# Linear attention, soft mixture of experts, ELU network: expert weights loaded by halves during the attention

## Chip, cores and metric

The kernel runs on one core of a Trainium2 chip. The metric is device time in microseconds, the median of several executions. The profile and the trace are those of one execution.

## The reference, cut to what matters

Three stages follow one another. The change touches the loads of `w1` and `w2`, which the second stage reads.

```python
# 1. linear attention: B, H, S, D = 4, 8, 768, 48
for t in range(S):
    cur = einsum('bhd,bhe->bhde', u * k[t], v[t])
    y[t] = einsum('bhd,bhde->bhe', r[t], state + cur)
    state = w * state + einsum('bhd,bhe->bhde', k[t], v[t])
# 2. soft MoE: x is 3072 x 384, 8 experts with 4 slots each, F = 1024
logits = x @ phi
d = softmax(logits, over tokens);  c = softmax(logits, over slots)
slot_input = d.T @ x
for e in range(8):
    slot_out[e] = relu(slot_input[e] @ w1[e]) @ w2[e]   # w1: 384x1024, w2: 1024x384
x = c @ slot_out
# 3. feed forward: 384 -> 2048 -> 384, w_in and w_out given as 64-bit floats
out = elu(x @ w_in) @ w_out
```

## The kernel before

The attention is computed in chunks of 128 rows, 24 of them (six for each of the four batches). One Python loop, `for s in range(-2, NCH)`, writes out the instructions of each step by hand, and every engine runs its own part of that list in order. In step s the kernel finishes chunk s, computes the scores of chunk s + 1 and prepares the keys of chunk s + 2. A step begins on TensorE with `update(s + 1)`, 16 small products at line 569 that read the values `vd` of chunk s + 1. They can therefore be used to see where a step begins. VectorE scales the keys, turns and masks the scores, adds the rows together and shifts bits in the conversion of `w_in` and `w_out` from 64-bit to 32-bit floats. The conversion (`wide_load`, `wide`) takes one piece of 384 columns in each of steps 0 to 19, through a scratch buffer `scr` of four pieces. The mixture's logits and slot sums for groups of four chunks are interleaved as `extras`.

All loads of this loop leave from SyncE's queue (SP), in the order in which the step lists them: `load_k(s + 4)`, after the keys of chunk s + 2 are scaled, as there are two key buffers; `load_v(s + 3)`; `wide_load(s + 2)`, one transfer of 384 KB or two smaller ones; `load_r`, 384 KB in every second step; and, at the end of some steps, weights of an expert. Keys and values are 192 KB in rows of 192 bytes, `r` is in rows of 384 bytes. The values of chunk s + 3 are thus asked for in step s and first read at the beginning of step s + 2.

There are sixteen expert matrices `we0` to `we15`: eight `w1`, each 128 x 3 x 1024 on the chip, and eight `w2`, each 128 x 8 x 384; 1.5 MB (12 KB per partition) apiece. The pool `we_p` has ten buffers, one of which is `scr`. The nine others take `we0` to `we8` during the attention. A whole matrix is issued at the end of steps 0, 3, 5, 7, 10, 12, 14, 17 and 19. The buffer is treated as 3072 columns, and a half of it is 1536. A half of a `w1` matrix does not end at the end of one of its three blocks of 1024 columns, so `load_half` (line 369 and line 374) needs two transfers for it: four for a matrix, of 512, 256, 256 and 512 KB, in rows of 4, 2, 2 and 4 KB. A half of a `w2` matrix is one transfer of 768 KB in rows of 1.5 KB. The rule for the step is:

```python
            if s >= 0 and s * (NWE - 1) // (NP + 1) >= nwe and nwe < NWE - 1:
                load_we(nwe, we_p)
                nwe += 1
```

with NWE = 10 and NP = 20. `we9` and the halves of `we10` follow in steps 21 and 22, the others after the attention, when buffers come free. After the attention `up` multiplies the slot inputs with four `w1` at a time (line 1048) and `down` with four `w2` (line 1070); both find a block through `we_at`.

Of the kernel before, what the change touches and what calls it, by code (L numbers as in the profile page):

```python
# [236 lines left out]
def kernel(  # L237
# [14 lines left out]
    nc = tc.nc  # L252
    B, H, S, D = r.shape
    E, DM, FE = w1.shape
# [7 lines left out]
    KD = DM // 128  # L262
    KF = FE // 128
# [15 lines left out]
    NWE = 10  # L279
    we_p = main.enter_context(tc.tile_pool(name="we_p", bufs=NWE, side="right"))  # L280
# [16 lines left out]
    for a in range(2):  # L297
# [5 lines left out]
        out=mask, in_=mask, compare_op=ALU.is_gt, fill=0.0, base=0, pattern=[[1, 128]], channel_multiplier=-1  # L303
# [45 lines left out]
    we = {}  # L349

    HW = KD * FE // 2

    def load_we(i, pool, part=None):
        if part in (None, 0):
            t = pool.tile([128, 2 * HW], F32, tag="we", name=f"we{i}")
            we[i] = [t[:, :HW], t[:, HW:]]
        for h in range(2) if part is None else [part]:
            load_half(i, h)

    def load_half(i, h):  # L360
        n = FE if i < E else DM
        src = (w1[i] if i < E else w2[i - E]).rearrange("(k p) f -> p k f", p=128)
        at = 0
        while at < HW:
            k, c = divmod(HW * h + at, n)
            m = min(HW - at, n - c)
            if c == 0 and m == n:
                m = (HW - at) // n
                nc.sync.dma_start(
                    out=we[i][h][:, at:at + n * m].rearrange("p (k f) -> p k f", k=m), in_=src[:, k:k + m]  # L370
                )
                at += n * m
            else:
                nc.sync.dma_start(out=we[i][h][:, at:at + m], in_=src[:, k, c:c + m])
                at += m

    def we_at(i, at, n):
        h, o = divmod(at, HW)
        return we[i][h][:, o:o + n]


# [16 lines left out]
    with ExitStack() as actx:  # L398
# [123 lines left out]
        def load_v(n):  # L522
            b, c = divmod(n, NC)
            vd[n] = at2.tile([128, H, D], F32, tag="vd", name="vd", bufs=4)
            nc.sync.dma_start(out=vd[n], in_=v[b, :, C * c:C * c + C, :].rearrange("h p d -> p h d"))

        def scale(n):
            nc.vector.tensor_tensor(out=km[:, :, 0:D], in0=rk.pop(n), in1=wk, op=ALU.mult)
# [37 lines left out]
        def update(n):  # L566
            for p in range(HP):
                for a in range(2):
                    nc.tensor.matmul(
                        out=pu[64 * a:64 * a + D, p, :], lhsT=km[:, 2 * p + a, 0:D], rhs=vd[n][:, 2 * p + a, :],  # L570
                        start=True, stop=True,
                    )
# [29 lines left out]
        def state(n):  # L602
            c = n % NC
            if c == NC - 1:
                return
            if c == 0:
                nc.vector.tensor_copy(out=t1, in_=pu)
            else:
                nc.vector.tensor_tensor(out=t1, in0=qc, in1=pu, op=ALU.add)
            nc.gpsimd.tensor_tensor(out=qc, in0=t1, in1=w128.unsqueeze(2).to_broadcast([128, HP, D]), op=ALU.mult)  # L610
# [73 lines left out]
        def logits(j, g0=0, g1=G):  # L684
            if g0 == 0:
                lg[j] = pm_p.tile([128, 128], F32, tag="pm", name="ps_l")
            for kk in range(KD):
                for g in range(g0, g1):
                    nc.tensor.matmul(
                        out=lg[j][32 * g:32 * g + 32, :], lhsT=phi_sb[:, kk, :], rhs=xT[G * j + g][:, kk, :],  # L690
                        start=(kk == 0), stop=(kk == KD - 1),
                    )
# [70 lines left out]
        def part(j):  # L763
            fs = [[logits], [slots_a], [], [slots_b], [slots_c], [slots_d], [slots_e], [slots_f], [], [], [], []]
            fs = [[(f, j) for f in l] for l in fs]

            def stage(l):
                for f, i in l:
                    f(i)

            return [lambda l=l: stage(l) for l in fs]
# [43 lines left out]
        NP = -(-NW // PW)  # L815
# [30 lines left out]
        def wide(j, f):  # L846
            if 0 <= j < NP:
                raw, a = piece(j)
                if f is not wide_d:
                    f(raw, a)  # L850
                    return
                merged = []
                for o, at, i, c, p, m in spans(j):
                    if merged and merged[-1][0] == o:
                        merged[-1][3] += m
                    else:
                        merged.append([o, at, p, m])
                for o, at, p, m in merged:
                    wide_d(raw[:, at:at + m, :], a[:, at:at + m], (wov if o else wiv)[:, p:p + m])
# [18 lines left out]
        load_r(1)  # L878
        load_k(1)
        load_v(1)  # L880
        nwe = 0
        extras = [lambda: None] * 7 + [flags_a, lambda: None, lambda: None, flags_b, lambda: None, flags_c, flags_d]

        def extra():
            if extras:
                extras.pop(0)()
# [3 lines left out]
        for s in range(-2, NCH):  # L890
            now, nxt, ahead = s >= 0, 0 <= s + 1 < NCH, s + 2 < NCH
            last = s == NCH - 1
            if nxt:
                update(s + 1)
            wide(s, wide_a)
            if last:
                extra()
                extra()
                extra()
                logits(GS - 1, 0, G - 1)  # L900
            else:
                extra()
            if s > 0 and s % G == 0:
                extras += part(s // G - 1)
            if nxt:
                state(s + 1)
            if ahead and s > -2:
                scale(s + 2)
            if 2 <= s + 4 < NCH:
                load_k(s + 4)  # L910
            if 2 <= s + 3 < NCH:
                load_v(s + 3)
            if s < 1:
                wide_load(s + 2)
            if now:
                for p in range(HP):
                    rows_a(s, p)
                rows_b(s)
                wide(s - 1, wide_d)
                if s >= 1 and s + 2 < NP:  # L920
                    wide_load(s + 2)
            if nxt:
                for p in range(HP):
                    scores(s + 1, p)
                causal(s + 1, 0)
                bonus_a(s + 1)
                bonus_c(s + 1)
            if not last:
                extra()
            turn_r(s + 3, k0 if s == -2 else rp)  # L930
            if s == -2:
                tables_b()
            if nxt:
                causal(s + 1, 1)
            if s % 2 == 0 and s // 2 + 3 < NCH // 2:
                load_r(s // 2 + 3)
            if now:
                x_T(s)
            if last:
                logits(GS - 1, G - 1, G)  # L940
            if nxt:
                bonus_b(s + 1)
            if ahead:
                ps = turn_k(s + 2)
            if nxt:
                bonus_d(s + 1)
            for f in (wide_b1, wide_b2, wide_b3):
                wide(s, f)
            if ahead:
                cross(s + 2, ps)  # L950
            wide(s, wide_c)
            if nxt:
                state_b(s + 1)
            spread(s + 4)
            if s == NCH - 2:
                warm(3)
            extra()
            if nxt:
                for p in range(HP):
                    before(s + 1, p)  # L960
            if s >= 0 and s * (NWE - 1) // (NP + 1) >= nwe and nwe < NWE - 1:
                load_we(nwe, we_p)
                nwe += 1
            if s == NP + 1:
                load_we(NWE - 1, we_p)
            if s >= NCH - 3 and not last:
                h = s - NCH + 3
                (rk_ctx, early)[h].close()
                pool = w2ctx.enter_context(tc.tile_pool(name=f"we2a{h}", bufs=1, side="right", reuse_waits="tile"))
                we.setdefault(NWE, []).append(pool.tile([128, HW], F32, name=f"we2a{h}"))  # L970
                load_half(NWE, h)
                nwe = NWE + h
# [54 lines left out]
    for a in range(2):  # L1027
        for q in range(4):
# [3 lines left out]
                out=s3, in_=s3, compare_op=ALU.is_ge, fill=0.0, base=-spe * e, pattern=[[1, NS]],  # L1032
# [3 lines left out]
                out=s3, in_=s3, compare_op=ALU.is_ge, fill=0.0, base=spe * e + spe - 1, pattern=[[-1, NS]],  # L1036
# [356 lines left out]
    for n in range(2, N + 3):  # L1393
# [4 lines left out]
        else:  # L1398
# [9 lines left out]
            j, h = divmod(steps.index(n), 2) if n in steps else (-1, 0)  # L1408
# [11 lines left out]
        else:  # L1420
            if n > HALF:
                outp(n - 3, (2, 3))
            if n == PAUSE[1]:
                leave(2)
                m = columns(CA, CB // 2)
# [42 lines left out]
```

## Time and profile before

| | |
|---|---|
| median of 3 runs | 437.71 us (435.57, 437.71, 440.0) |
| the profiled execution | 437.46 us, its span 435.3 us |
| TensorE busy in the span | 405.7 us (93%) |
| VectorE busy | 357.8 us (82%) |
| ScalarE busy | 269.7 us (62%) |
| GpSimd busy | 159.9 us (37%) |
| data moved | 57.44 MB |

The span runs from the first to the last instruction; the 2.2 us beside it are before and after. The busy shares are means over the whole span, and the three stages of the kernel have different limits. The attention takes about the first 150 us and nearly all of the loads; the feed-forward stage from about 190 us on moves little data.

### The profile page before, as it was taken

Reading aid. Unit: us, or ns where it says so; the run is one execution under the profiler, and the core shown is the slowest. Engines: PE = TensorE matmul, PEld = TensorE weight load, DVE = VectorE, ACT = ScalarE, POOL = GpSimd, SP = SyncE. Lnnn points to the kernel's source line nnn. Section 1 sums busy time; section 2 is a strip of 40 time slices with the busy share of each in tenths; the row PEclk is TensorE's granted clock in tenths of the full one; section 3 lists DMA queues with packets and bytes.
Section 4 is the critical chain, followed back from the end, with each engine's and each line's share of the span. In section 5 each row is a group of like instructions: output and inputs, shape, how many; then the busy total and the mean of one; then the engine's idle time right before and its main releaser. Section 6 shows DMA issues by size and latency. Waiting matters only on the chain.

```text
span 435.3 us, 10332 instructions
## 1 busy us (share of the span) xinstructions
PE 405.7 (93%) x4177; PEld 355.9 (82%) x4177; DVE 357.8 (82%) x573; ACT 269.7 (62%) x496; POOL 159.9 (37%) x170
## 2 busy tenths in 40 slices
PE   6998989999999979988999999999999899999994
PEld 5777777787777853457989999998989889999994
DVE  5998987999899645669889999997988988777762
ACT  3654654566464411657696878776778767767750
POOL 2365655565656207200004513530314124433340
PEclk9999989999999999999999999999999999999998
DMA  8989999999998886900001111110111002111122
GB/s 155 232 267 274 250 264 259 253 285 270 289 283 252 268 273 220 356 5 0 2 0 38 36 38 36 38 44 30 38 36 38 0 2 72 56 55 48 63 75 80
DMA packets 85097, 57.44 MB, mean 132 GB/s; under 512 B 65328, under 2 KB 76848, under 8 KB 85040
## 3 DMA queue, kind: packets, MB, share of 16 engines
q1 hardware_dynamic: 84224, 56.64, 45.2%
q8 instruction: 35, 0.57, 0.6%
q14 instruction: 22, 0.18, 0.1%
q10 hardware_dynamic: 816, 0.05, 0.1%
HBM read 51.96 MB, written 4.72 MB: 130 GB/s over the span
## 4 chain that ended last, share of the span: by engine, by line
PE 65%; DVE 17%; DMA 6%; ACT 5%; issue 5%; SPq 1%; POOL 1%; DVEq 0%; ACTq 0%; POOLq 0%
PE fo L1306 12%; PE fo L1309 12%; PE fo L1307 12%; PE fh L1261 4%; PE ps_a L582 4%; DMA vd<-in_v_dram 4%; PE py L657 3%; DVE ex L1275 3%; DVE ex L1280 2%; PE pd L1070 2%; PE ph L1048 2%; DVE rT L547 2%; PE py L643 2%; PE ps_k L533 2%; PE ps_r L533 2%
## 5 line engine op out<-in xcount | busy, mean ns | idle before, releaser
L1306 PE MATMUL fo<-wh,gh 128*128 128x384 f32 x384 | 130.3, 339 | 1.5 <-ACT gh L1288 1.0
L1307 PE MATMUL fo<-wl,gh 128*128 128x384 f32 x384 | 129.8, 338 | 0.0
L1309 PE MATMUL fo<-wh,gl 128*128 128x384 f32 x384 | 125.5, 339 | 3.3 <-DVE gl L1291 3.3
L1275 DVE SCALAR_TENSOR_TENSOR ex<-ex,th 128x1024 f32<-128x1024 f32 (+1 forms) x52 | 61.1, 1174 | 20.5 <-ACT ex L1272 20.3
L1306 PEld LDWEIGHTS fo<-wh,gh 128*128 128x128 f32 x384 | 72.2, 188 | 6.0 <-ACT acc L1243 2.4
L1309 PEld LDWEIGHTS fo<-wh,gl 128*128 128x128 f32 x384 | 71.8, 188 | 4.2 <-DVE gl L1291 4.2
L1269 ACT ACTIVATE th<-fh 128x1024 f32<-128x1024 f32 (+1 forms) x53 | 50.3, 950 | 38.3 <-PE fh L1261 38.3
L1307 PEld LDWEIGHTS fo<-wl,gh 128*128 128x128 f32 x384 | 72.2, 188 | 1.8
L1291 DVE TENSOR_TENSOR gl<-ex,gh 128x1024 fp32r<-128x1024 f32 (+1 forms) x52 | 68.4, 1315 | 1.7 <-ACT gh L1288 1.3
L337 POOL TENSOR_TENSOR cv<-raw,cv 128x384 f32<-128x384 f32 x12 | 19.4, 1617 | 132.3 <-ACT gh L1288 51.2
L1280 DVE SCALAR_TENSOR_TENSOR ex<-ex,fh 128x1024 f32<-128x1024 f32 (+1 forms) x52 | 58.8, 1132 | 0.5 <-ACT ex L1272 0.4
L1272 ACT ACTIVATE ex<-fh 128x1024 f32<-128x1024 f32 (+1 forms) x53 | 50.3, 949 | 9.6 <-DVE gl L1291 9.2
L1288 ACT CAST gh<-ex 128x1024 fp32r<-128x1024 f32 (+1 forms) x52 | 51.4, 988 | 6.3 <-DVE ex L1280 4.9
L1248 POOL TENSOR_TENSOR acc<-os,acc 128x384 f32<-128x384 f32 x20 | 26.9, 1359 | 43.8 <-ACT os L1247 43.8
L631 POOL TENSOR_TENSOR bv<-vd,bs 128x384 f32<-128x384 f32 x24 | 24.3, 1011 | 39.9 <-ACT bs L626 39.9
L586 DVE TENSOR_TENSOR am<-ps_a,mask 128x512 f32<-128x512 f32 x48 | 32.5, 681 | 2.4 <-PE ps_a L582 2.1
L1261 PE MATMUL fh<-cT,mst 128*128 128x512 f32 x96 | 30.6, 400 | 1.8 <-DVE mst L1188 1.1
L582 PE MATMUL ps_a<-rT,kT 64*128 64x128 f32 x384 | 28.3, 288 | 0.3 <-ACT kT L556 0.3
L657 PE MATMUL py<-vd,am 128*64 128x48 f32 x768 | 27.8, 226 | 0.4 <-DVE am L586 0.4
L657 PEld LDWEIGHTS py<-vd,am 128*64 128x64 f32 x768 | 25.4, 142 | 0.9 <-DVE am L586 0.7
L556 ACT COPY kT<-ps_k 128x512 f32<-128x512 f32 x24 | 14.1, 586 | 18.1 <-PE ps_k L533 18.1
L582 PEld LDWEIGHTS ps_a<-rT,kT 64*128 64x128 f32 x384 | 23.7, 191 | 1.7 <-ACT kT L556 0.4
(172 smaller groups left out, 650.2 us busy)
## 6 DMA issues: line engine op xcount, KB each, us to landing
we<-in_moe_w_dram SPq DMA_DIRECT2D x14, 768.0 KB, 7.7
we<-in_moe_w_dram SPq DMA_DIRECT2D x16, 512.0 KB, 6.5
rw<-in_r_dram SPq DMA_DIRECT2D x12, 384.0 KB, 5.0
rk<-in_k_dram SPq DMA_DIRECT2D x24, 192.0 KB, 4.7
vd<-in_v_dram SPq DMA_DIRECT2D x24, 192.0 KB, 5.3
out_dram<-acc SPq DMA_DIRECT2D x24, 192.0 KB, 1.9
we<-in_moe_w_dram SPq DMA_DIRECT2D x16, 256.0 KB, 6.0
scr<-in_moe_w_out_dram SPq DMA_DIRECT2D x10, 384.0 KB, 6.1
```

Of the source, the lines that this page charges most:

```text
L582: nc.tensor.matmul(out=aps[a][:, p, :], lhsT=kT[q, p, :], rhs=rT[n][q, p, :], start=True, stop=True)
L657: nc.tensor.matmul(out=py[q:q + 64, h, :], lhsT=am[n, a][:, p, q:q + 64], rhs=vd[n][:, h, :], start=(c == 0), stop=(c == 0 or h == H - 1),)
L1261: nc.tensor.matmul(out=ph[n][:, i, :], lhsT=mst[(f + i) // 8][:, 128 * ((f + i) % 8):128 * ((f + i) % 8) + 128], rhs=cT[:, TB * blk:TB * b ...
L1269: nc.scalar.activation(out=th[n][:, s], in_=ph[n][:, s], func=ACTF.Tanh, scale=0.5)
L1272: nc.scalar.activation(out=ex[n][:, s], in_=ph[n][:, s], func=ACTF.Exp)
L1275: nc.vector.scalar_tensor_tensor(out=ex[n][:, s], in0=ex[n][:, s], scalar=1.0, in1=th[n][:, s], op0=ALU.add, op1=ALU.mult)
L1280: nc.vector.scalar_tensor_tensor(out=ex[n][:, s], in0=ex[n][:, s], scalar=0.0, in1=ph[n][:, s], op0=ALU.min, op1=ALU.max)
L1288: nc.scalar.copy(out=gh[n][:, s], in_=ex[n][:, s])
L1291: nc.vector.tensor_tensor(out=gl[n][:, s], in0=ex[n][:, s], in1=gh[n][:, s].bitcast(F32), op=ALU.subtract)
L1306: nc.tensor.matmul(out=o, lhsT=gh[n][:, i, s], rhs=wh, start=(f == first), stop=False)
L1307: nc.tensor.matmul(out=o, lhsT=gh[n][:, i, s], rhs=wl, start=False, stop=False)
L1309: nc.tensor.matmul(out=o, lhsT=gl[n][:, i, s], rhs=wh, start=False, stop=(f == final))
```

## The change

The nine matrices are issued in eighteen halves. A half of a `w1` matrix is now made of columns: 512 of the 1024 columns of each of its three blocks. Each half is one transfer of 768 KB, with rows of 2 KB for `w1` and 1.5 KB for `w2`. `we_at` finds the block of 512 columns that `up` reads in the new place. At the end of a step one half is issued: in steps 0, 2 to 10 and 12 to 19. The parameter `queue` keeps its default everywhere, which is SP.

```diff
-    def load_we(i, pool, part=None):
+    def load_we(i, pool, part=None, queue=nc.sync):
...
-            load_half(i, h)
-
-    def load_half(i, h):
-        n = FE if i < E else DM
-        src = (w1[i] if i < E else w2[i - E]).rearrange("(k p) f -> p k f", p=128)
-        at = 0
-        while at < HW:
-            k, c = divmod(HW * h + at, n)
-            m = min(HW - at, n - c)
-            if c == 0 and m == n:
-                m = (HW - at) // n
-                nc.sync.dma_start(
-                    out=we[i][h][:, at:at + n * m].rearrange("p (k f) -> p k f", k=m), in_=src[:, k:k + m]
-                )
-                at += n * m
-            else:
-                nc.sync.dma_start(out=we[i][h][:, at:at + m], in_=src[:, k, c:c + m])
-                at += m
+            load_half(i, h, queue)
+
+    def load_half(i, h, queue=nc.sync):
+        o = we[i][h]
+        if i < E:
+            queue.dma_start(
+                out=o.rearrange("p (k f) -> p k f", k=KD),
+                in_=w1[i].rearrange("(k p) f -> p k f", p=128)[:, :, FE // 2 * h:FE // 2 * h + FE // 2],
+            )
+        else:
+            queue.dma_start(
+                out=o.rearrange("p (k f) -> p k f", f=DM),
+                in_=w2[i - E].rearrange("(k p) f -> p k f", p=128)[:, KF // 2 * h:KF // 2 * h + KF // 2, :],
+            )
...
-        h, o = divmod(at, HW)
+        if i < E:
+            kk, c = divmod(at, FE)
+            h, o = c // (FE // 2), FE // 2 * kk + c % (FE // 2)
+        else:
+            h, o = divmod(at, HW)
...
-            if s >= 0 and s * (NWE - 1) // (NP + 1) >= nwe and nwe < NWE - 1:
-                load_we(nwe, we_p)
-                nwe += 1
+            while s >= 0 and nhalf < min(2 * (NWE - 1), s * (NWE - 1) // 10 + 1):
+                load_we(nhalf // 2, we_p, nhalf % 2)
+                nhalf += 1
```

## Rows read from the trace of the kernel before

**Rows 1.** The page: DMA share in 40 slices; instruction reads (packets, MB, share)

```profile
DMA  8989999999998886900001111110111002111122
...
q8 instruction: 35, 0.57, 0.6%
```

**Rows 2.** Windows of the attention: engines busy, granted clock, DMA share, GB/s

```profile
10.00:60.00 50.00, 45.92 (x852) 37.94 (x852) 46.43 (x104) 28.61 (x77) 26.81 (x30) 1.00 0.98 259
60.00:70.00 10.00, 8.19 (x128) 7.02 (x128) 6.38 (x14) 3.67 (x10) 4.76 (x5) 0.83 0.97 244
70.00:150.00 80.00, 74.91 (x1457) 62.70 (x1460) 71.68 (x157) 45.99 (x132) 46.74 (x49) 1.00 0.97 275
```

**Rows 3.** Windows around 62 us, the same columns

```profile
62.00:64.00 2.00, 1.07 (x24) 1.07 (x26) 1.13 (x4) 0.74 (x3) 0.83 (x1) 0.74 1.13 266
64.00:66.00 2.00, 2.00 (x34) 1.91 (x32) 1.12 (x3) 0.98 (x2) 1.59 (x2) 0.50 0.84 140
66.00:68.00 2.00, 2.00 (x49) 1.68 (x45) 0.87 (x2) 0.27 (x1) 1.09 (x2) 0.90 0.94 253
```

**Rows 4.** Waits, 10 to 150 us: us in total, times, longest

```profile
PE pu L569 <- DMA vd<-in_v_dram: 1.9, 3, 1.2
ACT win L314 <- DMA scr<-in_moe_w_in_dram: 1.8, 2, 1.2
```

**Rows 5.** TensorE timeline, line 569: start us, us, idle before

```profile
38.13 0.53 PE L569 MATMUL pu<-vd,km 128*48 128x48 f32 x16
...
44.37 0.53 PE L569 MATMUL pu<-vd,km 128*48 128x48 f32 x16
...
55.83 0.53 PE L569 MATMUL pu<-vd,km 128*48 128x48 f32 x16
...
62.93 0.88 PE L569 MATMUL pu<-vd,km 128*48 128x48 f32 x16 [1.25 <-DMA vd<-in_v_dram]
...
70.71 0.53 PE L569 MATMUL pu<-vd,km 128*48 128x48 f32 x16
...
94.05 0.53 PE L569 MATMUL pu<-vd,km 128*48 128x48 f32 x16
...
99.87 0.53 PE L569 MATMUL pu<-vd,km 128*48 128x48 f32 x16
...
106.52 0.56 PE L569 MATMUL pu<-vd,km 128*48 128x48 f32 x16 [0.27 <-DMA vd<-in_v_dram]
...
112.14 0.53 PE L569 MATMUL pu<-vd,km 128*48 128x48 f32 x16
...
118.92 0.56 PE L569 MATMUL pu<-vd,km 128*48 128x48 f32 x16 [0.37 <-DMA vd<-in_v_dram]
```

**Rows 6.** SyncE timeline: start us, us taken to issue

```profile
53.45 0.43 SPq L369 DMA_DIRECT2D we<-in_moe_w_dram  x1
53.99 0.38 SPq L520 DMA_DIRECT2D rk<-in_k_dram  x1
54.87 1.34 SPq L525 DMA_DIRECT2D vd<-in_v_dram  x1
```

**Rows 7.** DMA issues near 54 us: KB each, us to landing

```profile
we<-in_moe_w_dram SPq DMA_DIRECT2D x1, 512.0 KB, 6.3
...
rk<-in_k_dram SPq DMA_DIRECT2D x1, 192.0 KB, 6.5
...
vd<-in_v_dram SPq DMA_DIRECT2D x1, 192.0 KB, 8.0
```

**Rows 8.** Windows with 2 KB rows, 4 KB rows and 192-byte rows in transfer

```profile
100.20:100.50 0.30, 0.30 (x20) 0.30 (x16) 0.30 (x2) 0.28 (x2) 0.30 (x1) 1.00 1.07 403
101.40:101.90 0.50, 0.50 (x10) 0.50 (x12) 0.50 (x2) 0.50 (x2) 0.10 (x1) 1.00 1.04 393
102.50:103.20 0.70, 0.70 (x16) 0.22 (x9) 0.69 (x2) 0.27 (x1) 0.70 (x1) 1.00 1.20 273
```

**Rows 9.** Chain that ended last: the first expert product

```profile
162.53 5.34 PE ph L1048 x46
```

More of the change, by code (lines that the diff above doesn't have):

```diff
@@ L880 @@
         load_v(1)
-        nwe = 0
+        nwe, nhalf = 0, 0
         extras = [lambda: None] * 7 + [flags_a, lambda: None, lambda: None, flags_b, lambda: None, flags_c, flags_d]
```

## The prediction

> **What bounds the kernel now.** I first read where loads and arithmetic lie beside each other. The DMA engines work at nine tenths in the first fourteen slices, which are the attention, and at one or two tenths from slice 18 on [rows 1]: a change of loads in the attention can cost or gain time there alone. In the windows of the attention VectorE is busy 46.43 of 50 us and 71.68 of 80 us, TensorE 45.92 and 74.91 [rows 2]. So the steps run at VectorE's pace, with TensorE close behind; the ten steps from 55.83 to 118.92 us [rows 5] last 6.31 us on average. The DMA share beside them is 0.97 to 0.98, and has to be read with care: where only rows of 192 bytes are under way it reads 1.20, where only large rows are, 1.04 to 1.07 [rows 8], since rows overlap on an engine. A full queue would read about 1.1 in the mix, so 0.97 is a queue filled to some 88%.
>
> The one window that falls out is 60 to 70 us: VectorE works 6.38 us of 10, and TensorE's granted clock is 0.83 [rows 2]. The step timeline says why. `update` waited 1.25 us for its values at 62.93, and 0.27 and 0.37 us at 106.52 and 118.92 [rows 5]; these three are all the 1.9 us that TensorE waits for values in the waits [rows 4]. ScalarE waited for pieces of `w_in` as well, 1.8 us in two waits, the longest 1.2 us [rows 4]. After the first of these waits the granted clock falls: 0.74, 0.50 and 0.90 in three windows of 2 us [rows 3], which means that the lower of the two levels, 1.2 GHz, held in between.
>
> Now the cause of that wait. The last quarter of `we2` was issued at 53.45, the keys at 53.99 and the late values at 54.87 [rows 6]; they landed 6.3, 6.5 and 8.0 us later [rows 7], at 59.75, 60.5 and 62.9. Transfers of one queue land in order here, so the values stood behind the whole of `we2`, which left at the end of step 5. The two other late values, of chunks 16 and 18, were also asked for in the step after a matrix (steps 12 and 14). That is the pattern: a matrix of 1.57 MB, at 393 GB/s [rows 8] 4.0 us of transfer, stands in front of the next step's keys and values, and then one or two steps have no weights at all.
>
> A second thing helped. Keys and values landed 2.4 us apart, where 197 KB at 273 GB/s [rows 8] take 0.72. The 35 instruction reads take 0.6% of 16 engines [rows 1]: 0.006 x 16 x 435.3 / 35 = 1.2 us each, on one engine. An engine so held is late with its share of whatever stands behind. They come with and without the change.
>
> **The change, part by part.** *Halves, one per step.* With one half fewer in front, what is behind it lands 0.786 MB / 393 GB/s = 2.0 us earlier. Counting halves issued by the end of each step, the new order is one behind the old after steps 0, 1, 3, 5, 7, 12 and 14, equal after most others, and one ahead after steps 9, 16 and 18. All three late values (asked for in steps 6, 13 and 15) are behind one half fewer. TensorE was ready for the first at 62.93 - 1.25 = 61.68; it would land at 60.9, 0.8 us before. The other two would come 1.6 to 1.7 us early. What is next late is then VectorE's own work.
>
> What this is worth I read by comparing a step with one of the same place in its batch (six steps later or before), so that the work is alike. The step that ends at 62.93 lasts 7.10 us against 5.82 (94.05 to 99.87): 1.28. The next, 7.78 against 6.65 - 0.27 = 6.38 (99.87 to 106.52): 1.40, the slow clock; by the windows the clock took 2 x (0.26 + 0.50 + 0.10) = 1.72 us of TensorE's full speed [rows 3], part of which VectorE's slack hides. The wait at 106.52: 0.27. The step that ends at 118.92, 6.78 against 6.24 (38.13 to 44.37): 0.54 [rows 5]. Together 3.5 us. With ScalarE's other wait, 1.8 - 1.2 = 0.6 us, which may be hidden, it is 4.1 at most; the TensorE waits alone, without the clock, are 1.9. I take 3.5.
>
> *What is moved past what.* The second half of each matrix that keeps its first step is moved past the next step's keys, values and conversion piece on SP; these leave earlier. In steps 9, 16 and 18 a half is moved ahead, before the keys and values of steps 10, 17 and 19, which land 2.0 us later; in rows none of those three was waited for. The values for steps 13, 20 and 22 have no bracket in the timeline, and the waits list only three. No engine but SP issues any of it, so GpSimd's and ScalarE's queues don't change. Weights are read only after the attention, at 162.53 the first time [rows 9], and the last half still leaves in step 19: nothing waits for them.
>
> *One transfer for a half.* Sixteen issues fewer on SP (four to two for each of eight `w1`), at 0.43 us [rows 6] 7 us of a queue that only matters where it is late. I count nothing. *Rows of 2 KB.* Two thirds of each `w1`, 8.4 MB in all, go from rows of 4 KB to rows of 2 KB. Where 2 KB rows were under way the trace moved 403 GB/s at a share of 1.07, with 4 KB rows 393 at 1.04 [rows 8]: per busy share 377 against 378. By the shares alone rows of 2 KB would be 3% dearer (0.03 x 8.4 MB / 393 GB/s = 0.6 us in the whole attention), by the rates alone 2.5% cheaper (0.5 us). I take 0, as the two together say; either end lies within the slack of the queue.
>
> The Trainium skill speaks against this part: Perfetto Trace Analysis, "DMA Optimizations", says that batching transfers from 2 KB up to 4 or 8 KB can raise throughput dramatically when the kernel is bound by DMA. This kernel's windows don't bear that out for rows of 2 KB, 403 against 393 GB/s.
>
> *Is there room in every step?* Keys 0.72, values 0.72, a piece of 0.39 MB 1.0, half of `r` 0.72, half a matrix 2.0: 5.2 us of queue in a step that then lasts 6.31 - 0.35 = 5.96 us. An instruction read of 1.2 us in a step fills it to 6.4 for that step only.
>
> *`we_at`.* The products read the same number of columns from another place: 0.
>
> Sum: 437.46 - 3.5 = 434.0 us against the profiled execution, which lies 0.25 us under the median of the runs; I keep 434.0. A change of 1% is 4.4 us, the distance between the lowest and the highest of the runs before, and about what a measurement of this kernel can tell from no change.
>
> **The rivals.** *A late value stays (436.7).* The 1.7 us by which values lagged their keys exceed the 0.8 us margin that I found; if an instruction read hits the same place with a later queue, one wait and its slow clock stay: 434.0 + 1.28 + 1.40. For it: the reads come all along. Against it: three waits in some twenty steps.
>
> *The queue is the bound (436.0).* If a share of 0.97 to 0.98 means full, only what is missing in the windows from 10 to 150 us can be won, 0.02 x 50 + 0.03 x 90 = 3.7 us if every gap closes, and rows of 2 KB cost up to 0.6 of it: between 434.4 and 437.5. I put the middle, 436.0. This is the case in which the rule of the skill named above would count. Against it: VectorE without idle time in the windows [rows 2], and shares of 1.20 where the queue is surely full.
>
> *No light step is left (441).* In the old order the steps after a burst, without weights, let the queue recover; now each step but two has a half. Place: the values of every step. It decides from the point at which a step's queue work passes 5.96 us: with the values at 2.4 us, as seen once, instead of 0.72, it is 6.9. If one step in three of the eighteen is so hit, six waits at the mean price of the three seen, 3.5 / 3 = 1.17 us, cost 7.0: 434.0 + 7.0 = 441.0. For it: no reserve beside the weights except in steps 1 and 11. Against it: 5.2 us of work, and the old bursts recovered within a step or two.
>
> *It doesn't do what it says*: a transfer with three runs per partition might be issued slowly or be cut up. The `w2` halves already are one transfer of four runs; I give it 2 in 100, with no gain, 437.5.
>
> **How the numbers follow.** The forecast, 432.8 to 435.2, has 0.54; a late value that stays 0.18, the full queue 0.14, no light step 0.12, and 0.02 for the last. The range reaches from 431.8 (all 4.1 us and one more wait of a run that the profile didn't see, 437.46 - 4.1 - 1.5) to 438.2: it leaves out the case without light steps and a little below. Faster by over 1% is below 433.3: that is a part of the forecast's case, half of it, and a little for what other executions lose, 0.30. Slower by over 1% is above 442.1: somewhat over half of the case without light steps, 0.07. The rest, 0.63.
>
> **What would show it.** In the timeline of the changed kernel line 569 should carry no bracket for values, the window in the 60s should have VectorE above 9 us of 10 and a clock of 1.00, and the waits should have no row of TensorE for values. The eighteen halves should land 2.0 us after what is in front of them. The DMA share should stay at 0.97. The prediction is wrong if brackets stand in steps 9 to 12 or 17 to 19, if halves of `w1` take over 2.2 us, or if steps without any wait still last 6.3 us.

## The result and the profile after

The changed kernel takes 441.45 us in the median of four runs (440.26 to 442.99), the kernel before 436.75 us beside it: a ratio of 1.012, with an interval from 1.0083 to 1.0158. It is 1.2% slower, and above the range of the prediction. The profiled execution took 440.26 us, its span is 438.2 us at a granted clock of 0.997; the span before was 435.3.

The windows of the attention, with the columns of [rows 2]:

```profile
10.00:60.00 50.00, 45.92 (x852) 37.95 (x852) 46.46 (x104) 28.53 (x77) 26.87 (x30) 1.00 0.98 252
60.00:70.00 10.00, 9.45 (x206) 8.45 (x208) 8.98 (x22) 5.96 (x18) 5.80 (x7) 1.00 1.01 278
70.00:150.00 80.00, 71.39 (x1366) 59.21 (x1364) 69.15 (x148) 43.89 (x126) 45.55 (x48) 1.00 0.98 270
```

The middle window is what the prediction asked for: VectorE 8.98 us of 10 where it had 6.38, and a clock of 1.00 where it had 0.83 [rows 2]. The last window is the opposite: VectorE does 69.15 us of work where it did 71.68, TensorE 71.39 where it did 74.91. The DMA share says nothing about it (0.98 after, 0.97 before).

The timeline of TensorE, line 569, the start of a step (columns of [rows 5]):

```profile
61.50 0.53 PE L569 MATMUL pu<-vd,km 128*48 128x48 f32 x16
...
79.77 0.53 PE L569 MATMUL pu<-vd,km 128*48 128x48 f32 x16
85.69 0.56 PE L569 MATMUL pu<-vd,km 128*48 128x48 f32 x16 [0.76 <-DMA vd<-in_v_dram]
93.26 0.56 PE L569 MATMUL pu<-vd,km 128*48 128x48 f32 x16 [1.12 <-DMA vd<-in_v_dram]
...
117.63 0.56 PE L569 MATMUL pu<-vd,km 128*48 128x48 f32 x16 [0.19 <-DMA vd<-in_v_dram]
123.93 0.56 PE L569 MATMUL pu<-vd,km 128*48 128x48 f32 x16 [1.07 <-DMA vd<-in_v_dram]
131.28 0.56 PE L569 MATMUL pu<-vd,km 128*48 128x48 f32 x16 [0.92 <-DMA vd<-in_v_dram]
```

The late value at 62.93 [rows 5] is gone: its step now starts at 61.50. At update 12 (79.77; 82.75 before) the new kernel is 2.98 us ahead. Then it gives everything back in five waits. The waits between 10 and 150 us (us in total, times, longest) beside [rows 4]:

```profile
ACT wo L314 <- DMA scr<-in_moe_w_out_dram: 5.4, 6, 1.5
PEld pu L569 <- DMA vd<-in_v_dram: 5.1, 5, 1.3
...
PE pu L569 <- DMA vd<-in_v_dram: 4.1, 5, 1.1
```

TensorE waits 4.1 us for values where it waited 1.9, and ScalarE 5.4 us for pieces of `w_out` where it waited 1.8 for pieces of `w_in` [rows 4] and 0.3 for pieces of `w_out`. Update 23 begins at 148.09 us (147.34 before), and the first expert product, in the chain that ended last, at 163.28 (162.53, [rows 9]). The attention is thus 0.75 us longer. This distance stays up to the last product of the kernel, which ends at 430.46 us (429.70 before).

But the span is 2.9 us longer. The other 2.15 us come after the last product. SyncE's waits from 425 to 440 us show them; first after, then before:

```profile
SPq L1436 <- SPq L1436: 4.8, 2, 2.7
```

```profile
SPq L1436 <- SPq L1436: 2.6, 1, 2.6
```

Line 1436 is the jump over a second path through the kernel that never runs. Each program waits some 2.6 us at this jump. The changed one stands still a second time behind it, for 4.8 - 2.7 = 2.1 us, and an 8 KB instruction read of queue 14 starts within each of the two pauses (431.91 and 434.37 us). The pages count one read more on that queue; first after, then before:

```profile
q14 instruction: 23, 0.19, 0.1%
```

```profile
q14 instruction: 22, 0.18, 0.1%
```

### The profile page after: what moved, and what is told of

The parts are those of the page before. It is cut to its first block, busy times and chain, and to the rows that moved or that the text cites. A ratio compares the mean times of both kernels' runs of the same rounds, so it can differ in the third digit from the quotient of the medians.

```text
span 438.2 us, 10318 instructions
## 1 busy us (share of the span) xinstructions
PE 404.3 (92%) x4177; PEld 354.4 (81%) x4177; DVE 358.1 (82%) x573; ACT 269.9 (62%) x496; POOL 159.9 (36%) x170
## 4 chain that ended last, share of the span: by engine, by line
PE 63%; DVE 19%; DMA 6%; ACT 5%; issue 5%; POOL 0%; DVEq 0%; ACTq 0%; SPq 0%
PE fo L1306 12%; PE fo L1309 12%; PE fo L1307 12%; PE fh L1261 4%; PE ps_a L582 4%; DMA vd<-in_v_dram 3%; PE py L657 3%; DVE rT L547 3%; DVE ex L1275 3%; DVE ex L1280 2%; PE pd L1070 2%; PE ph L1048 2%; DVE am L586 2%; DMA scr<-in_moe_w_out_dram 2%; PE py L643 2%
## 5 line engine op out<-in xcount | busy, mean ns | idle before, releaser
L586 DVE TENSOR_TENSOR am<-ps_a,mask 128x512 f32<-128x512 f32 x48 | 32.5, 682 | 2.5 <-PE ps_a L582 2.3
L657 PE MATMUL py<-vd,am 128*64 128x48 f32 x768 | 26.9, 222 | 0.4 <-DVE am L586 0.4
L678 ACT COPY xT<-ps_x 128x384 f32<-128x384 f32 x24 | 11.5, 478 | 21.5 <-PE ps_x L676 21.4
```

Source lines behind the costliest of these rows:

```text
L657: nc.tensor.matmul(out=py[q:q + 64, h, :], lhsT=am[n, a][:, p, q:q + 64], rhs=vd[n][:, h, :], start=(c == 0), stop=(c == 0 or h == H - 1),)
```

## The experiments

Two things had to be told apart first. The theory for the end: SyncE's program has 16 instructions fewer ahead of the place jumped to, so this place lies otherwise in the blocks in which its instructions are read; loads and arithmetic have no part in it. Its rival: a chance of one execution. The theory for the attention: one half in *every* step stands in front of the next keys and values, and no step is left in which SyncE and its queue catch up. Its rival: the new form of the transfers (one of 768 KB in rows of 2 KB) is dearer than counted.

**The program's end, and one part of the change at a time.** These four ran beside the same runs of the kernel before (median 435.63 us). `e1` and `e4` repeat the loads of `w` in the path that never runs, which lies ahead of the place jumped to and so brings back SyncE's old length, to within an instruction:

```diff
             nc.sync.dma_start(out=wt[H * i:H * i + H, :], in_=w)
+            nc.sync.dma_start(out=wt[H * i:H * i + H, :], in_=w)
```

> The changed kernel with 17 more SyncE instructions in the fallback branch that never runs; nothing that executes is different, but the branch's target at the end of SyncE's program lies 17 instructions further. Theory A, the place of the program's end: the 2.1 us in which SyncE stands still between two semaphore instructions after the last output (434.34 to 436.43 us in the trace after) are a read of the next block of its program, and go: 439.3 us, 5.0 us from the end of VectorE's last addition to the end of the span, not 7.1. Theory B, the whole loss is in the attention: 441.4 us as after, the gap stays.

`e2` is the kernel before, shortened in that path alone:

```diff
-            nc.sync.dma_start(out=wt[H * i:H * i + H, :], in_=w)
+            if i == 0:
+                nc.sync.dma_start(out=wt[H * i:H * i + H, :], in_=w)
```

> The kernel before with 15 SyncE loads less in the fallback branch that never runs (the fallback would be wrong, it isn't taken); the loads of the attention are untouched. Theory A: the end of SyncE's program comes to lie as it does in the changed kernel, a stop of 2.1 us appears among its last semaphore instructions, 438.9 us. Theory B: 436.8 us as before, no stop.

`e3` is the change with the old `load_half` and `we_at`: new order, old transfers.

> The new order (a half per step) with the old transfers (halves of 1536 columns, two transfers for a half of w1, rows of 4 and 2 KB); SyncE has as many instructions as before, so its end lies as before. If the order causes the attention's loss (values late from step 12 on): 439.3 us, waits for values at the end of steps 12, 13, 17, 18 and 19 as after. If the format does: 436.8 us or, by the forecast's step, 434.0. If both only together: between.

`e4` is the change with the old rule: whole matrices at the old steps, each as two transfers of the new form.

```diff
-            while s >= 0 and nhalf < min(2 * (NWE - 1), s * (NWE - 1) // 10 + 1):
-                load_we(nhalf // 2, we_p, nhalf % 2)
-                nhalf += 1
+            if s >= 0 and s * (NWE - 1) // (NP + 1) >= nwe and nwe < NWE - 1:
+                load_we(nwe, we_p)
+                nwe += 1
```

> The old order (whole matrices) with the new transfers (one of 768 KB for a half, w1 by columns in rows of 2 KB), and the fallback branch longer by 17 SyncE instructions so that the program's end lies as before. If the order causes the attention's loss: 436.8 us, with the wait near 62 us and its slow clock as before. If the format does, each half of w1 takes over 2.5 us and the time is 439.3 us.

| kernel | median us | ratio, interval | update 23 in the profile | after the last VectorE work |
|---|---|---|---|---|
| e1, change padded | 440.71 | 1.011 (1.0074 to 1.0145) | 149.6 | 5.3 us |
| e2, before shortened | 438.72 | 1.0086 (1.0054 to 1.0118) | 144.35 | 7.2 us |
| e3, order alone | 439.07 | 1.008 (1.0057 to 1.0103) | 152.89 | 5.0 us |
| e4, form alone | 436.96 | 1.0052 (1.0024 to 1.008) | 145.7 | 5.1 us |

The pause at the end follows the length of the program: the shortened kernel before has it. SyncE's waits from 425 us on, in `e2`:

```profile
SPq L1437 <- SPq L1437: 4.9, 2, 2.8
```

The padded change has hardly any of it (3.0 us there, longest 2.7). In all runs kept here queue 14 has 23 reads where the pause is (the change, `e2`, `e12`) and 22 where it isn't. But the ratio of the padded change, 1.011, is hardly better than the change's 1.012. In its profiled execution the attention was longer in turn: a value came 1.4 us late, and the granted clock read 0.89, 0.50 and 0.76 in the windows of 2 us from 92 us on. So this pair doesn't price the pause; a later one does. `e2` is 3.1 us above its runs of before, one more than the pause; that one stays open.

For the attention, the order alone costs 0.8%, and the form alone 0.5%, with intervals that overlap. The trace of `e3` has the waits for values of the changed kernel, and more of them; the profiled execution, 443.24 us, is the longest of its seven:

```profile
PEld pu L569 <- DMA vd<-in_v_dram: 7.5, 7, 1.5
PE pu L569 <- DMA vd<-in_v_dram: 5.8, 5, 1.4
ACT wo L314 <- DMA scr<-in_moe_w_out_dram: 5.8, 6, 1.7
```

`e4`, in an execution of 435.97 us, has 0.5 us of TensorE's waits for values and 3.2 us of ScalarE's for pieces of `w_out`. The order looks like the main part, but the times alone don't show it.

`e2` showed something else. Its attention is that of the kernel before, instruction for instruction, and update 23 starts at 144.35 us, 3.0 us earlier than in the profile that the prediction was made from. In that execution, the shortest of its six (436.25 us), update 9 begins at 61.48 us without a wait.

**Where does the order lose?** SyncE's timeline of the changed kernel (start, us taken to issue):

```profile
78.19 0.43 SPq L363 DMA_DIRECT2D we<-in_moe_w_dram  x1
78.71 0.44 SPq L520 DMA_DIRECT2D rk<-in_k_dram  x1
79.25 0.52 SPq L525 DMA_DIRECT2D vd<-in_v_dram  x1
79.88 4.21 SPq L839 DMA_DIRECT2D scr<-in_moe_w_out_dram  x1
84.18 0.39 SPq L508 DMA_DIRECT2D rw<-in_r_dram  x1
84.62 0.57 SPq L363 DMA_DIRECT2D we<-in_moe_w_dram  x1
85.29 0.44 SPq L520 DMA_DIRECT2D rk<-in_k_dram  x1
85.83 1.38 SPq L525 DMA_DIRECT2D vd<-in_v_dram  x1
87.30 4.36 SPq L839 DMA_DIRECT2D scr<-in_moe_w_out_dram  x1
91.76 0.39 SPq L520 DMA_DIRECT2D rk<-in_k_dram  x1
```

An issue takes about 0.4 us when there is room in the queue. The fourth transfer in a row, the piece of the conversion behind a half, keys and values, takes over 4 us here, during which SyncE issues nothing. Added up over the issues begun from 56 to 132 us, SyncE is busy issuing for 72.2 of 76 us in the changed kernel (10 of its 11 pieces over 2 us), against 67.3 before (6 of 12). No step has a pause left: each step's loads leave when SyncE gets to them and not when the step asks for them.

It comes too late for the DMA engines as well. The windows of the changed kernel before and after the end of the long issue (columns of [rows 2]):

```profile
79.00:84.00 5.00, 4.74 (x98) 4.01 (x96) 4.93 (x13) 2.68 (x7) 2.76 (x4) 1.00 1.03 301
84.00:84.90 0.90, 0.62 (x4) 0.42 (x4) 0.90 (x3) 0.14 (x1) 0.90 (x1) 1.00 0.53 70
...
91.20:92.40 1.20, 0.94 (x18) 0.69 (x16) 1.13 (x5) 0.97 (x4) 0.25 (x1) 1.00 0.45 71
```

Where the issue that began at 79.88 ends, at 84.09, the engines fall to 70 GB/s; after the one of 87.30 to 91.66 they fall to 71. The queue was nearly empty before SyncE could fill it again. Such holes are short, and the mean share of 0.98 hides them. Other kernels below have them too, so a hole by itself isn't yet the loss. So there were three suspects: SyncE itself, the half's place in front of the values, and the amount of data. The next kernels, all padded, ran beside one set of runs of before (median 436.13 us), or beside a second set (436.23 us) for `e9` to `e11`.

**Another queue.** `e5` issues the halves from ScalarE's queue, `e7` the old whole matrices; the edit of `e5`:

```diff
-                load_we(nhalf // 2, we_p, nhalf % 2)
+                load_we(nhalf // 2, we_p, nhalf % 2, nc.scalar)
```

> The changed kernel with the eighteen halves issued from ScalarE's queue in place of SyncE's, at the same place of each step; the fallback branch is longer so that SyncE's program ends as before. Bytes and rows are the same. Theory C, one queue in order: SyncE's queue holds some two thousand rows; a half in front of 2048 rows of keys and values makes the next piece's issue wait until about 600 small rows are left, and the DMA engines run dry; with the weights in a queue of their own that ends: no wait for values, steps 8 to 20 at VectorE's pace (5.96 us on average), 433.5 us, with 18 x 0.5 us of issuing on ScalarE hidden. Theory D, the DMA engines' rate itself: the same bytes in the same steps, values late from step 12 on, 440 us.

> The old order (whole matrices, two transfers of 768 KB each) from ScalarE's queue, padded. Theory C: as with the halves on ScalarE's queue, 433.5 us, or a little more where 4 us of weights share the engines with the values: 434. Theory D: as the format alone, 437 us.

`e5`: 436.93 us, 1.0015 (0.9983 to 1.0048). `e7`: 439.16 us, 1.0057 (1.0026 to 1.0087). The first lies between the two theories' times, the second above both. SyncE's issues in `e5` fall to 56.6 of 76 us and its loads fall behind less (the values of chunk 12 leave at 71.11 us, in the changed kernel at 73.55), but the waits of `e5` show values late in three steps all the same:

```profile
PEld pu L571 <- DMA vd<-in_v_dram: 3.6, 3, 1.7
...
PE pu L571 <- DMA vd<-in_v_dram: 3.0, 3, 1.5
...
ACT wo L316 <- DMA scr<-in_moe_w_out_dram: 2.8, 2, 1.6
```

With whole matrices it is worse, one wait of 2.7 us. On a queue of its own a weight is no longer in front of the values, it is beside them. The Trainium skill, DMA: Bandwidth & Descriptors, "Queues, rings and completion order", says that each engine goes round the queues that have work; the late values agree with that, though no run here separates its packets. The halves on this queue give back most of the loss (1.0015, where the padded change has 1.011). Whole matrices give back nothing (1.0057, and 1.0052 from SyncE's queue in `e4`). SyncE issues the values of `e5` in better time and three are late all the same, so it wasn't SyncE's issuing alone.

**Another place.** `e6` issues the half one step later, between the values and the piece:

```diff
             if 2 <= s + 3 < NCH:
                 load_v(s + 3)
+            while s >= 1 and nhalf < min(2 * (NWE - 1), (s - 1) * (NWE - 1) // 10 + 1):
+                load_we(nhalf // 2, we_p, nhalf % 2)
+                nhalf += 1
...
-            while s >= 0 and nhalf < min(2 * (NWE - 1), s * (NWE - 1) // 10 + 1):
-                load_we(nhalf // 2, we_p, nhalf % 2)
-                nhalf += 1
```

> The changed kernel with each half issued one step later, between the values and the conversion piece, so that the next keys and values stand behind a piece and r alone; the fallback branch is padded. Theory C: keys and values (2048 rows) now fill the queue in front of the half, the half's issue waits instead of the piece's, the engines still run dry once per step: 438 us, values late by less. Theory D: the mean work is the same, values still fall behind step by step, 440 us. If only the half in front of the values mattered: 434 us.

437.49 us, 1.0041 (1.0003 to 1.0078). TensorE's waits for values all but vanish, and the pieces are late in their place:

```profile
ACT wo L315 <- DMA scr<-in_moe_w_out_dram: 9.7, 10, 1.6
...
PEld pu L570 <- DMA vd<-in_v_dram: 0.5, 2, 0.3
```

**Less data.** `e8` leaves out twelve of the eighteen halves:

```diff
-                load_we(nhalf // 2, we_p, nhalf % 2)
+                load_we(nhalf // 2, we_p, nhalf % 2, skip=nhalf // 2 in (1, 2, 3, 5, 6, 7))
```

> The changed kernel without the loads of w1 of experts 1 to 3 and 5 to 7 in the attention (12 of 18 halves left out; experts 0 and 4 stand in for them, so the result is wrong), padded. It gives the attention's own pace: values never waited for, steps at VectorE's pace, 433.5 us by both theories. If the steps stay at 6.3 us and more, the weights aren't what makes them late.

433.26 us, 0.9923 (0.9894 to 0.9952), no wait of TensorE for values, update 23 at 143.50 us. This is taken as the attention's own pace, and so as a floor for any order of these loads: 4.6 us under the changed kernel's 148.09, and 0.85 under `e2`.

**The values earlier.** `e9` asks for values one chunk further ahead, at the end of the step and just in front of the half; all else is the change, padded. `e10` does the same to the kernel before.

```diff
-            if 2 <= s + 3 < NCH:
-                load_v(s + 3)
...
+            if 2 <= s + 4 < NCH:
+                load_v(s + 4)
             while s >= 0 and nhalf < min(2 * (NWE - 1), s * (NWE - 1) // 10 + 1):
```

> The changed kernel with the load of the values moved: those of chunk s + 4 are issued at the end of step s, just in front of the half, in place of those of chunk s + 3 early in step s; four value buffers are still enough, as chunk s is done by then. Padded. If a half in front of the values is the whole loss: 434 us, no wait for values. Theory C, SyncE's blocked issues (the queue then holds values, half, keys and piece, still over two thousand rows): values in time, but the keys and pieces fall behind by half a microsecond a step, ScalarE waits for pieces in most steps from step 12 on, 437 us.

> The kernel before with the same move of the values, in front of the whole matrix. By both: no values late, the light steps let keys and pieces recover, and the attention runs nearly at its own pace: 434 us, in all executions within 1 us. If this is as slow as the kernel before, the values behind a matrix aren't what costs time there.

`e9`: 433.69 us (433.12 to 434.48), 0.995 (0.9929 to 0.997); update 23 at 143.53. It has the bytes, transfers, halves and steps of the change, and runs at the floor; it is faster than both kernels. The padded change, from which it differs in the values alone, has 1.011. What I had feared, late pieces and 437 us, didn't come: its waits have no row for pieces. Its windows at the place of the hole above:

```profile
79.00:84.00 5.00, 4.72 (x98) 4.01 (x96) 4.93 (x12) 2.62 (x7) 2.77 (x4) 1.00 1.16 274
84.00:84.90 0.90, 0.72 (x9) 0.55 (x11) 0.90 (x3) 0.13 (x1) 0.90 (x1) 1.00 0.85 295
```

and SyncE's timeline behind it:

```profile
83.88 0.53 SPq L840 DMA_DIRECT2D scr<-in_moe_w_out_dram  x1
84.51 0.90 SPq L526 DMA_DIRECT2D vd<-in_v_dram  x1
87.86 0.37 SPq L521 DMA_DIRECT2D rk<-in_k_dram  x1
88.33 1.11 SPq L840 DMA_DIRECT2D scr<-in_moe_w_out_dram  x1
89.53 0.39 SPq L509 DMA_DIRECT2D rw<-in_r_dram  x1
90.02 0.52 SPq L526 DMA_DIRECT2D vd<-in_v_dram  x1
90.59 1.76 SPq L364 DMA_DIRECT2D we<-in_moe_w_dram  x1
93.65 0.37 SPq L521 DMA_DIRECT2D rk<-in_k_dram  x1
```

No hole here, and SyncE has pauses again (85.41 to 87.86 in the step without a half, 92.35 to 93.65 in one with a half), though it still issues for 62.5 of 76 us. It has holes elsewhere, 91 GB/s from 123.5 to 125.0 us, and loses nothing by them: the values of chunk 20, which the next step reads, were asked for at 113.35 us and took 8.0 to land. A half, blocked or not, now stands between the values of one step and the keys of the next, where SyncE has to wait for the step anyway.

`e10`: 434.28 us (433.71 to 438.95), 0.997 (0.9946 to 0.9994). The old order gains from it too, but keeps some long executions, and not all lie within 1 us as expected: in the profiled one, the longest of 13, ScalarE waits for pieces behind matrices, 7.1 us in three waits for `w_out`. Between `e9` and `e10` the medians don't decide.

**Shorter to issue.** `e11` is the padded change with keys read in 128 rows of 1,536 bytes in place of rows of 192:

```diff
-            nc.sync.dma_start(out=rk[n], in_=k[b, :, C * c:C * c + C, :].rearrange("h p d -> p h d"))
+            nc.sync.dma_start(out=rk[n].rearrange("p h d -> p (h d)"), in_=k[b].rearrange("h s d -> (h s) d").rearrange("(c p j) d -> c p (j d)", p=C, j=H)[c])
```

> The changed kernel, padded, with the keys of a chunk read as 128 rows of 1536 bytes that lie together in memory, in place of 1024 rows of 192 (other keys than the reference's, so the result is wrong; the bytes are the same). A half, keys, values and piece are then 1664 rows, not 2560, and fit into SyncE's queue. Theory C: no issue of SyncE over 2 us in the steady steps, values asked for at the same point of each step, none late, 434 us. Theory D, rate: the keys take 0.5 us, not 0.72, so 20 steps gain 4 us of queue at most; the values still fall behind, by less, 437 us.

433.69 us, 0.995 (0.9928 to 0.9972), update 23 at 143.5: the floor again, with the values still behind a half in every step. Its bytes are the change's; only the rows of the keys are fewer, by seven eighths. SyncE's issues fall to 32.5 of 76 us and no piece takes 2 us; two halves still do, 3.1 and 2.7 us. Its steps keep time with the changed kernel's up to update 12 (79.78 and 79.77 us), so the same load can be compared in both. The values of chunk 13, which update 13 needs, first in `e11`, then in the changed kernel (start and us taken; KB, us to landing):

```profile
76.87 0.65 SPq L526 DMA_DIRECT2D vd<-in_v_dram  x1
...
vd<-in_v_dram SPq DMA_DIRECT2D x1, 192.0 KB, 3.9
```

```profile
79.25 0.52 SPq L525 DMA_DIRECT2D vd<-in_v_dram  x1
...
vd<-in_v_dram SPq DMA_DIRECT2D x1, 192.0 KB, 6.4
```

They land at 80.8 and at 85.7 us, where `e11` needs them at 84.80. Of the 4.9 us between, 2.4 are SyncE asking later, and 2.5 the longer way through the queue. Fewer rows also leave the engines some time (their share from 10 to 150 us is 0.92 where the change has 0.98), so the run doesn't price the blocking alone. Rows issued and packets ended can be counted in the two traces, from 50 to 135 us. With under 1,000 rows outstanding an issue took 0.6 us on average in the changed kernel and 0.4 in `e11`, with over 2,200 it took 3.1 and 2.9; the changed kernel has 15 of 58 issues of this second kind, `e11` 2 of 60. So the blocking goes with the rows that are outstanding. And the run shows that the place behind the half doesn't cost by its 2 us of transfer: it costs together with the many short rows that keep SyncE and the queue full.

**The price of the end.** `e12` is `e9` without the padding; it ran beside a third set of runs of before (435.45 us).

> The changed kernel with the values issued a step earlier, just before the half, as in the experiment that ran at 433.7 us and a ratio of 0.995, but without the 17 loads added to the part of the program that never runs. Theory: the 2.1 us in which SyncE stands still at the end of the profiled execution of the changed kernel come from the length of SyncE's program alone; then SyncE has a gap of about 2.1 us after the last matmul here too, update 23 still begins at 143.5 us, and the median is about 435.8 us, a ratio of 0.999 to 1.001. Rival: the gap is a chance of one execution; then the time is 433.7 us and the ratio 0.995.

435.75 us (435.63 to 436.39), 0.9999 (0.9981 to 1.0017), update 23 at 143.5. SyncE's waits from 425 to 440 us in `e12` and in `e9`:

```profile
SPq L1436 <- SPq L1436: 4.7, 2, 2.6
```

```profile
SPq L1437 <- SPq L1437: 2.6, 1, 2.6
```

The pause of 2.1 us (4.7 - 2.6) follows the length of the program, and the medians of the two differ by just that, 435.75 - 433.69 = 2.06 us; no run of the one reaches into the range of the other. Here it is shown in the time too.

## Why the prediction was wrong

*What is this worth: 3.5 us.* For the execution that it was read from, the size is right: update 23 began at 147.34 us there, 3.8 above the 143.50 of `e8`. What failed is the step from that execution to the kernel. The same attention in `e2`, in the shortest of its executions, starts update 23 at 144.35: 3.0 us less, with no late value at update 9. So the 61.50 in place of 62.93 isn't shown to be the change's doing either. The three sets of runs beside `e1` to `e11` have medians of 435.63 to 436.23 us, 1.2 to 1.8 under the execution that I built the sum on; 8 of the 29 runs beside `e9` are longer than it, so such executions aren't rare. By the medians of `e9` and its runs of before, 436.23 - 433.69 = 2.5 us were to be won by a better order, not 3.5, and not by this one.

*Is there room in every step: 5.2 us of 5.96.* This is the step that cost the time. The sum itself isn't refuted: `e9` moves the same bytes in the same steps and runs at the floor. What failed is what was read from it, that a load lands once the transfers in front of it are through, and leaves when its step asks for it. The time to issue was put at nothing: "7 us of a queue that only matters where it is late" went by issues of 0.4 us, as in [rows 6]. In the changed kernel the 11 pieces take 3.4 us each to issue (37.2 us in all), and SyncE is busy issuing for 72.2 of 76 us, so loads leave late; then they stand in a queue that is full. For the values of chunk 13 that made 2.4 and 2.5 us. The long issues were in the trace of before as well (29.5 us for 12 pieces, 6 over 2 us), where steps without weights came in between.

*No light step is left (441).* This rival had the place and nearly the time: values late in five waits, the longest 1.1 us, where it had six of 1.17 us each. That its 441.0 is so near 441.45 is partly luck: some 2.1 us of the measured time are the pause at the end, of which it knew nothing. How much is open, as the padded change, without the pause, took 440.71 us beside other runs. Its point of decision, queue work over 5.96 us, was wrong. `e9` carries the same work in the same steps and `e11` the same bytes, and neither loses anything.

*In steps 9, 16 and 18 a half is moved ahead; none of those values was waited for.* The old cover was a step or two without weights behind each matrix, as the rival said; with it gone, the values at 85.69, 93.26, 117.63, 123.93 and 131.28 came late. These begin steps 12, 13, 17, 18 and 19, about where the prediction had said that brackets would prove it wrong. ScalarE's waits for pieces, 1.8 us of which I had 0.6 as a possible gain, rose to 5.4.

*Sixteen issues fewer: nothing.* Their time to issue was looked at, but not the length of the program: 2.1 us at the end, by `e12` against `e9`.

*Rows of 2 KB: 0.* Not settled. The form alone was 1.0052 (1.0024 to 1.008), so 1 to 3.5 us and not 0; its profile shows 0.5 us of waits for values and update 23 1.4 us after `e2`. A matrix in the new form has more rows (768 where it had 512), which would block SyncE sooner, but no run separates this from the size of the transfers. The rule that the prediction weighed (the Trainium skill, Perfetto Trace Analysis, "DMA Optimizations") points the same way, and stays as open.

The sum as the runs have it, in the profiles: from `e2`'s 144.35 us the change loses 3.7 us in the attention (148.09) and 2.1 us at the end. Against the profiled execution of before, which had lost 3.0 in its own attention, 0.75 + 2.15 = 2.9 us remain. The executions of the change and of `e2` are the shortest of their runs. By medians, which come from different sets of runs, the change lies 441.45 - 438.72 = 2.7 us above `e2`, and the padded change `e1` 440.71 - 433.69 = 7.0 us above `e11`, so the attention's loss is known to a few us only.

## What to carry to other kernels

Before a stall becomes a gain, look how many other executions have it: a median gains only in the measure in which they do. Price a queue by its issuing engine too: add up the issue times in the timeline, and where an engine has no pause left, ask which load stands behind the one that blocks, and move the needed load ahead of it. Compare two versions of a program only with the same number of instructions ahead of a place jumped to, or two microseconds of layout pass for an effect of the change.

## What the hardware showed that I had not expected

- A jump at the end of a program cost SyncE 2.1 us more when its program was 17 instructions shorter, and nothing else differed (`e12` and `e9`: 435.75 and 433.69 us). The Trainium skill, Runtime: NRT & Kernel Launch, "Instruction fetch mechanics", says that a taken branch whose target isn't in the stretch of the program at hand has to wait until that stretch is fetched. The trace agrees, with 2.6 us of SyncE's waits at line 1437 in `e9`. That the place of the target can add a second stop, 4.7 us in all at line 1436 in `e12`, is what these two runs show beyond it.
- An issue of one transfer, 0.4 us with room in the queue, took up to 4.4 us behind a half, keys and values, and the engines were down to 70 GB/s before the next one could start. Keys in rows of 1,536 bytes in place of 192 ended that for the pieces (32.5 us of issuing in all in place of 72.2).
- Weights on a second queue didn't leave the values alone: three came late in `e5`, by up to 1.5 us.
